# The opening of a fused attention and gated-FFN kernel: root scratch in PSUM, scalings on ScalarE, another order of the first loads, fewer warm-up matmuls

## The chip, the cores and the metric

The kernel runs on one core of one Trainium2 chip, as a single program with one launch. The metric is the device time of one execution in microseconds (us). The core has five engines with queues of their own, each worked off in order: TensorE (PE in the profile; PEld is its weight load), VectorE (DVE), ScalarE (ACT), GpSimd (POOL) and SyncE (SP), which here only issues DMAs. ACT issues a few DMAs too.

## What is computed

The input x is one sequence of 2048 tokens of width 512 in float32. It is normalised (mean and variance of a token, without gain), and two branches work on the result: attention with 32 heads of 16 columns and a window of 256 tokens, and a gated FFN of width 1792. Cut to its core, the reference is:

```python
xn = (x - mean(x)) / sqrt(var(x) + 1e-5)
q, k, v = split(xn @ wqkv)                 # 32 heads of 16
p = softmax(where(0 <= i - j < 256, q @ k.T / 4, -1e9))
s = (p @ v) @ wo
g = silu((silu(xn @ w_gate) * (xn @ w_up)) @ w_down)
out = x + s * g
```

## The kernel before

**Arithmetic.** Every float32 operand of a dense product is split in two parts of the format float32r: a high part (ACT casts it) and a low part, the difference (POOL for weights, DVE for what comes out of PSUM). Three products are made of them, high by high, high by low and low by high. All dense matmuls stand on line 580 (`mm`). In names, `wr` is a raw weight tile, `wh` and `wl` its parts, `xh` and `xl` those of x, and `xt` a raw tile of 128 tokens by 512 columns.

**Two halves.** PE's 128 rows are used as two halves of 64 that work on different matmuls at the same time. A unit of dense work (`vp` values, `a` queries and keys, `g` and `u` gate and up, `d` down, `s` the output product) runs on its lower half first (row half 0), and later the other 64 rows add into the same PSUM bank (row half 1). Between them stands a handover, line 577: a one-column copy by DVE that reads the bank after half 0 has finished, and for which half 1's first matmul waits. Half 0 of a unit uses the lower rows of its weight tile, half 1 the upper rows of the next tile.

**The order.** The whole program is straight-line code written by a planner in Python: it keeps a virtual clock, estimated costs of each instruction (`do`, `dma`) and due times, and emits each instruction when the virtual clock says that its inputs are there. The order on each engine is fixed by it; on the chip an engine waits only at semaphores. Dense units come from a list that `dense_order` sorts with the constant `LEAD`; attention work (`b` row maxima, `mt` and `ms` their turn and negation, `c` scores, `pv`) is slotted between by due times that are counted in dense work less the same `LEAD`.

**The opening.** `load_first` (line 320) fetches the first 512 tokens as four tiles `xt` in row halves over the queues of SP and ACT, and the first weights, those of the value product (`wr0`, `wr1`). DVE takes mean and variance of each tile (lines 338 and 339); the tiles are centred, two by ACT (346) and two by DVE (343). PE turns the centred tiles with matmuls against an identity (`x_turn`, line 442) into PSUM banks `xp`, ACT casts the high part (465), DVE subtracts for the low part (462). The value product of these centred, not yet scaled tokens starts at once, and its result is scaled when it leaves PSUM (838). Meanwhile DVE finds the reciprocal root of the four variances: two `tensor_scalar` for variance plus epsilon (`ve`, 362) and its half (`hv`, 363), an integer shift and subtraction for a first guess (364, 365), and three Newton steps of three instructions each (370 to 372), all on 128 x 4 elements. Then the x tiles are scaled (two by DVE on 387, two by ACT on 385) and turned once more in 64-row halves (`xt_turn`, line 600) for all later products. Until the first x tile is there, PE runs matmuls on a constant tile (`warm_up`, line 242): 20 at the start, 3 and 5 more behind the first two turns. A float32 matmul of this kind shows as two passes in the profile.

**The constants.** Three key buffers need rows of ones. `constants2` fetches them by nine DMAs from a tile of ones (`k<-one`) on SP's queue. Weights after the first come by `w_fetch`, a chain that begins at virtual time 4.0.

## Time and profile before

| | us |
|---|---|
| median of 3 runs | 863.81 (863.65 to 864.82) |
| the profiled execution, its own time | 866.53 |
| its span in the profile | 864.4 |
| PE busy | 852.1 |
| DVE, ACT, POOL busy | 509.7, 484.9, 627.2 |
| mean granted TensorE clock | 0.994 |

The profiled execution took 2.1 us more than its span, and 2.7 us more than the median of the runs without a profile. "Busy" counts the time in which at least one matmul was in work, so a PE that runs on one half of its rows counts as fully busy. In the views, a row of the timeline gives start, length, engine, line, operation, what is written and read, shapes, and in brackets the idle time before it with what ended it. A row of the windows gives the stretch, its length, the busy time with the number of instructions, the granted TensorE clock, the DMA share and GB/s.

### The profile page before, as it was taken

To read this page: it belongs to the slowest core of one execution; us is meant where nothing else is said; L and a number is where in the kernel's file an instruction comes from. 1 tells how busy PE (TensorE), PEld (TensorE's weight loads), DVE (VectorE), ACT (ScalarE), POOL (GpSimd) and SP (SyncE) were. 2 spreads that over 40 slices of the span, in tenths; PEclk is the share of its full clock that TensorE was granted. 3 is DMA by queue.
4 is the path that set the end of the run, shared out by engine and by line. 5 is a ranking of instruction groups with operands and counts; after the bars stand their busy time and mean duration, and the time that the engine had idled before them with its cause. 6 is when DMAs were issued, how large, how long until landed. Compare 5 with 4: busy or idle time off the path is not lost.

```text
span 864.4 us, 30040 instructions
## 1 busy us (share of the span) xinstructions
PE 852.1 (99%) x11976; PEld 794.6 (92%) x11976; DVE 509.7 (59%) x1672; ACT 484.9 (56%) x966; POOL 627.2 (73%) x906
## 2 busy tenths in 40 slices
PE   7999999999999999999999999999999999999997
PEld 7998988889999989989999998999999999999897
DVE  6337576655766565756657776566555576653234
ACT  4624755655666447655566656565546665665430
POOL 6535867877777587868787788667677877888770
PEclk9999999999999999999999999999999999999999
DMA  7279847475876986487758977666777778845241
GB/s 180 76 177 186 214 117 195 126 197 128 184 172 163 240 210 156 89 204 167 185 112 196 224 188 182 137 167 139 178 173 195 148 179 175 193 109 139 79 132 50
DMA packets 69550, 139.61 MB, mean 162 GB/s; under 512 B 14610, under 2 KB 23314, under 8 KB 69412
## 3 DMA queue, kind: packets, MB, share of 16 engines
q1 hardware_dynamic: 69092, 137.18, 66.4%
q8 instruction: 94, 1.54, 0.8%
q10 hardware_dynamic: 320, 0.52, 0.2%
q14 instruction: 44, 0.36, 0.2%
HBM read 107.74 MB, written 29.62 MB: 159 GB/s over the span
## 4 chain that ended last, share of the span: by engine, by line
PE 89%; DMA 7%; DVE 1%; SPq 1%; ACT 0%; issue 0%; POOL 0%; ACTq 0%; POOLq 0%; DVEq 0%
PE u L580 17%; PE d L580 17%; PE g L580 17%; PE a L580 10%; PE pv L1285 8%; PE c L1248 6%; PE b L1100 5%; PE vp L580 5%; PE s L580 4%; DMA xt<-x 1%; SPq L100 1%; DMA r<-rd 1%; DMA out<-y 1%; DMA qkd<-qkl 1%; DMA q<-ms 1%; DMA wr<-wv 1%
## 5 line engine op out<-in xcount | busy, mean ns | idle before, releaser
L545 POOL TENSOR_TENSOR wl<-wr,wh 128x512 fp32r<-128x512 f32 (+2 forms) x258 | 304.5, 1195 | 94.9 <-ACT wh L541 81.5
L1108 DVE CUSTOM_DVE_ANT_0 jk<-b,maskb 128x384 bf16<-128x384 f32 (+2 forms) x512 | 271.6, 530 | 103.1 <-PE b L1100 50.5
L580 PE MATMUL d<-wh,hh 64*128 64x256 f32 x1792 | 262.1, 278 | 0.0
L1208 ACT ACTIVATE p<-c 128x512 f32<-128x512 f32 (+2 forms) x384 | 197.6, 571 | 98.9 <-PE c L1248 95.0
L580 PEld LDWEIGHTS d<-wh,hh 64*128 64x128 f32 x1792 | 227.6, 185 | 1.1 <-issue 0.6
L580 PE MATMUL d<-wl,hh 64*128 64x256 f32 x896 | 208.4, 278 | 0.0
L580 PE MATMUL u<-xh,wl 64*128 64x512 f32 x448 | 168.3, 394 | 0.0
L580 PE MATMUL u<-xh,wh 64*128 64x512 f32 x448 | 168.2, 396 | 0.0
L580 PE MATMUL g<-xh,wh 64*128 64x512 f32 x448 | 166.5, 394 | 1.2 <-DVE ho L577 1.2
L580 PE MATMUL u<-xl,wh 64*128 64x512 f32 x448 | 167.1, 394 | 0.0
L580 PE MATMUL g<-xl,wh 64*128 64x512 f32 x448 | 167.0, 395 | 0.0
L580 PE MATMUL g<-xh,wl 64*128 64x512 f32 x448 | 167.0, 394 | 0.0
L541 ACT ACTIVATE wh<-wr 128x512 fp32r<-128x512 f32 (+2 forms) x258 | 142.5, 589 | 36.7 <-DMA wr<-wgu 20.4
L580 PEld LDWEIGHTS d<-wl,hh 64*128 64x128 f32 x896 | 152.5, 185 | 0.7 <-issue 0.2
L1220 POOL TENSOR_SCALAR_AFFINE_SELECT p<-p 128x256 f32<-128x256 f32 x256 | 101.9, 410 | 25.0 <-ACT p L1208 24.8
L1100 PE MATMUL b<-k,q 48*128 48x384 f32 (+2 forms) x512 | 113.0, 328 | 1.2 <-ACT ms L1149 0.7
L1224 POOL TENSOR_SCALAR_AFFINE_SELECT p<-p 128x256 f32<-128x256 f32 x224 | 91.5, 409 | 28.5 <-ACT p L1208 28.2
L735 POOL TENSOR_TENSOR hh<-h,hh 128x512 fp32r<-128x512 f32 x56 | 72.4, 1293 | 36.9 <-ACT hh L731 36.8
L1248 PE MATMUL c<-q,k 49*128 49x128 f32 (+2 forms) x704 | 96.0, 299 | 0.2 <-DMA q<-ms 0.2
L580 PE MATMUL a<-xh,wh 64*128 64x512 f32 x256 | 95.2, 393 | 0.0
L580 PE MATMUL a<-xh,wl 64*128 64x512 f32 x256 | 95.2, 392 | 0.0
L580 PE MATMUL a<-xl,wh 64*128 64x512 f32 x256 | 94.9, 392 | 0.0
(112 smaller groups left out, 2154.9 us busy)
## 6 DMA issues: line engine op xcount, KB each, us to landing
wr<-wgu SPq DMA_DIRECT2D x112, 256.0 KB
k<-qkd SPq DMA_DIRECT2D x48, 192.0 KB
wr<-wqk SPq DMA_DIRECT2D x32, 256.0 KB
qkd<-qkh SPq DMA_DIRECT2D x32, 256.0 KB
qkd<-qkl SPq DMA_DIRECT2D x32, 256.0 KB
q<-qkd SPq DMA_DIRECT2D x64, 128.0 KB
wr<-wdn SPq DMA_DIRECT2D x32, 256.0 KB
od<-ev SPq DMA_DIRECT2D x32, 256.0 KB
```

The source lines that it names most:

```text
L100: eng.dma_start(dst, src)
L541: nc.scalar.activation(wtile[j][0][pr, a:b], raw[pr, a:b], AF.Copy)
L545: nc.gpsimd.tensor_tensor(lo[pr, a:b], raw[pr, a:b], f32(hi[pr, a:b]), op=ALU.subtract)
L580: return nc.tensor.matmul(pb, a, b, start=first, stop=last, skip_group_check=True)
L735: nc.gpsimd.tensor_tensor(hl[:, 1, :], self.h, f32(hl[:, 0, :]), op=ALU.subtract)
L1100: nc.tensor.matmul(pb[:, :n], qs[u % 3][r : r + 48, p, qb * P : (qb + 1) * P], ks[u % 3][r : r + 48, p, lo : lo + n], start=True, stop=True,)
L1108: nc.vector.tensor_tensor_reduce(junk[:, :n], pb[:, :n], maskb[:, 3 * P - n :], 1.0, -3.0e38, ALU.add, ALU.max, m[:, col : col + 1],)
L1208: nc.scalar.activation(t[:, h, :], pc[:, :n], AF.Exp, scale=DH ** -0.5)
L1220: nc.gpsimd.affine_select(s, s, [[0, 2], [1, P]], ALU.is_ge, 0.0, base=0, channel_multiplier=-1)
L1224: nc.gpsimd.affine_select(s, s, [[0, 2], [-1, P]], ALU.is_gt, 0.0, base=0, channel_multiplier=1)
L1248: nc.tensor.matmul(pc[:, at0 : at0 + w], ks[u % 3][r : r + 49, p, k0 : k0 + P], qs[u % 3][r : r + 49, p, qb * P : qb * P + w], start=(i == ...
L1285: nc.tensor.matmul(pbs[r][0][32 * j : 32 * j + 32, q0:q1], vt[half(r), (4 * c + kb) % VT, VW * (4 * g + j) : VW * (4 * g + j) + 32], t[hal ...
```

## The change

In words, from top to bottom of the diff:

- `LEAD` goes from 0.9 to 1.1, which moves units in the dense list and attention work between them, over the whole run.
- The rows of ones are fetched by three DMAs of 2 x 3 x 512 elements in place of nine of 2 x 512.
- The scratch of the roots (`ve`, `tm` and the running root `r1`) lies in the PSUM bank of the warm-ups, `wbank`; `hv`, a new product tile `t1` and the finished root `rs` lie in SBUF.
- Of the four x tiles, three are centred on ACT and one on DVE; all four are scaled on ACT.
- The first weight tile's lower rows come in two column halves, one on ACT's queue and one on SP's, ahead of the third x tile; the fourth x tile and the upper rows of the second weight tile come over SP alone, the latter in column halves.
- The third and fourth x tile are turned into banks of the dense pool (`fb_free`) in place of the attention pool (`rb_free`).
- Warm-ups go from 20, 3 and 5 to 11, 1 and 2, and the weight chain begins at virtual time 6.5.
- The planner's numbers for landings, engines and lanes in the opening are changed with them.

```diff
@@ -50,7 +50,7 @@
 PRIO = -0.5
 MM = 0.2315
 PACE = 17.6
-LEAD = 0.9
+LEAD = 1.1
 OUT = 2.4
 STEP = 0.05
 LAND = 3.5
@@ -212,17 +212,17 @@
         for t in mts:
             nc.gpsimd.memset(t, 0.0)
 
-        def ones(t, b):
+        def ones(t):
             k = t[48 : 113 : 64].rearrange("p a n -> p (a n)")
-            move(k[:, b * 512 : b * 512 + 512], one[:2])
+            move(k.rearrange("p (b n) -> p b n", b=3), one[:2].unsqueeze(1).to_broadcast([2, 3, 512]))
 
         def done(t, i):
             ones_at[i] = t
-            if i == 8:
+            if i == 2:
                 timer(t, give, one)
 
-        for i in range(9):
-            dma(max(now[0], 1.1), lambda i=i: ones(ks[i // 3], i % 3), lambda t, i=i: done(t, i), 4.0, 8)
+        for i in range(3):
+            dma(max(now[0], 1.1), lambda i=i: ones(ks[i]), lambda t, i=i: done(t, i), 4.0, 8)
         nc.gpsimd.memset(vt[:, :, : H * VW].rearrange("p t (h c) -> p t h c", c=VW)[:, :, :, DH], 1.0)
         nc.gpsimd.memset(vt[:, :, H * VW :], 1.0)
 
@@ -318,18 +318,19 @@
     first = {}
 
     def load_first():
-        mv, ve, rs, tm, nm = (
+        mv, rs, nm = (
             pers.tile([P, 4, 2] if n == "mv" else [P, 4], F32, name=f"{n}0", tag=n)
-            for n in ("mv", "ve", "rs", "tm", "nm")
+            for n in ("mv", "rs", "nm")
         )
-        hv = pers.tile([P, 4], F32, name="hv")
+        hv, t1 = (pers.tile([P, 4], F32, name=n) for n in ("hv", "t1"))
+        ve, tm, r1 = (wbank[:, 256 + 4 * n : 260 + 4 * n] for n in range(3))
         first["rs"] = rs
         left = [4]
-        lands = (3.7, 4.7, 6.8, 7.8)
-
-        def rows(i):
+        lands = (3.8, 4.75, 6.4, 7.3)
+
+        def rows(i, upper):
             xt[0, i] = take(f"xt0_{i}")
-            for r, eng in ((0, nc.sync), (1, nc.scalar)):
+            for r, eng in ((1, upper), (0, nc.sync)):
                 at = i * P + R * r
                 move(xt[0, i][half(r)], x[at : at + R, :], eng)
 
@@ -337,7 +338,7 @@
             st = sb(f"st0_{i}", [P, 6], F32, "st", 2)
             nc.vector.bn_stats(st, xt[0, i])
             nc.vector.bn_aggr(mv[:, i, :], st)
-            if i % 2 == 0:
+            if i != 1:
                 nc.vector.tensor_scalar(nm[:, i : i + 1], mv[:, i, 0:1], -1.0, None, op0=ALU.mult)
             else:
                 nc.vector.tensor_scalar(xt[0, i], xt[0, i], mv[:, i, 0:1], None, op0=ALU.subtract)
@@ -349,8 +350,8 @@
             turns[i] = t
 
         def after_stats(t, i):
-            if i % 2 == 0:
-                do("S", t, 0.55, lambda: center(i), lambda t: centered(t, i), -1.0)
+            if i != 1:
+                do("S", t, 0.6, lambda: center(i), lambda t: centered(t, i), -1.0)
             else:
                 centered(t, i)
             left[0] -= 1
@@ -363,28 +364,25 @@
             nc.vector.tensor_scalar(hv, mv[:, :, 1], EPS, -0.5, op0=ALU.add, op1=ALU.mult)
             nc.vector.tensor_scalar(tm.bitcast(i32), ve.bitcast(i32), 1, None, op0=ALU.logical_shift_right)
             nc.vector.tensor_scalar(
-                rs.bitcast(i32), tm.bitcast(i32), -1, 0x5F3759DF, op0=ALU.mult, op1=ALU.add
+                r1.bitcast(i32), tm.bitcast(i32), -1, 0x5F3759DF, op0=ALU.mult, op1=ALU.add
             )
 
-        def newton():
-            nc.vector.tensor_tensor(tm, rs, hv, op=ALU.mult)
-            nc.vector.tensor_tensor(tm, rs, tm, op=ALU.mult)
-            nc.vector.scalar_tensor_tensor(rs, tm, 1.5, rs, op0=ALU.add, op1=ALU.mult)
+        def newton(n):
+            nc.vector.tensor_tensor(t1, r1, hv, op=ALU.mult)
+            nc.vector.tensor_tensor(t1, r1, t1, op=ALU.mult)
+            nc.vector.scalar_tensor_tensor(rs if n == 2 else r1, t1, 1.5, r1, op0=ALU.add, op1=ALU.mult)
 
         def step(t, n):
             if n < 3:
-                do("V", t, 0.6, newton, lambda t: step(t, n + 1), -0.5)
+                do("V", t, 0.6, lambda: newton(n), lambda t: step(t, n + 1), -0.5)
                 return
             rsready.append(t)
+            rb_free[wtag] = t
             for i in range(4):
-                e = "S" if i % 2 else "V"
-                do(e, t, 0.55, lambda i=i: scale(i), lambda t, i=i: normed.__setitem__((0, i), t), 0.1 * i)
+                do("S", t, 0.6, lambda i=i: scale(i), lambda t, i=i: normed.__setitem__((0, i), t), 0.1 * i)
 
         def scale(i):
-            if i % 2:
-                nc.scalar.activation(xt[0, i], xt[0, i], AF.Identity, scale=rs[:, i : i + 1])
-            else:
-                nc.vector.tensor_scalar(xt[0, i], xt[0, i], rs[:, i : i + 1], None, op0=ALU.mult)
+            nc.scalar.activation(xt[0, i], xt[0, i], AF.Identity, scale=rs[:, i : i + 1])
 
         def split(raw, j, r, t):
 
@@ -414,29 +412,32 @@
 
                 do("S", t, 0.53, lambda a=a: high(a), done, 0.3 + 0.001 * a)
 
-        rows(0)
-        rows(1)
+        rows(0, nc.scalar)
+        rows(1, nc.scalar)
         wr = [w_take(f"wr{j}", F32) for j in range(2)]
         u0, u1 = weighted[0], weighted[1]
-        for t, r, u, at in ((wr[0], 0, u0, 0), (wr[1], 1, u0, 1)):
-            move(t[half(r), : u.width], u.src[half(r)])
-        rows(2)
-        rows(3)
+        for a, eng in ((512, nc.scalar), (0, nc.sync)):
+            move(wr[0][half(0), a : a + 512], u0.src[half(0), a : a + 512], eng)
+        rows(2, nc.scalar)
+        rows(3, nc.sync)
+        for a in (0, 512):
+            move(wr[1][half(1), a : a + 512], u0.src[half(1), a : a + 512])
         move(wr[1][half(0), : u1.width], u1.src[half(0)])
         split_next[0] = 2
-        free_at["D"] = free_at["S"] = 4.0
-        stream_at[0] = 5.0
-        lanes[:] = [5.2, 5.8, 6.8, 6.8, 7.8, 7.8, 8.3, 8.3]
+        free_at["D"] = 6.8
+        free_at["S"] = 4.7
+        stream_at[0] = 5.7
+        lanes[:] = [5.4, 6.3, 6.4, 7.2, 7.3, 7.8, 8.2, 9.2]
         for i in range(4):
-            do("V", lands[i], 1.05 if i % 2 == 0 else 1.45, lambda i=i: stats(i), lambda t, i=i: after_stats(t, i), -1.0)
-        split(wr[0], 0, 0, 5.3)
-        split(wr[1], 1, 1, 7.2)
-        split(wr[1], 1, 0, 8.5)
+            do("V", lands[i], 1.05 if i != 1 else 1.45, lambda i=i: stats(i), lambda t, i=i: after_stats(t, i), -1.0)
+        split(wr[0], 0, 0, 5.5)
+        split(wr[1], 1, 1, 8.3)
+        split(wr[1], 1, 0, 9.3)
 
     def x_turn(i):
         h = i // 2
         if i % 2 == 0:
-            first["ab"[h]] = [bank(rb_free, f"xp0_{2 * h + n}") for n in range(2)]
+            first["ab"[h]] = [bank(fb_free if h else rb_free, f"xp0_{2 * h + n}") for n in range(2)]
         for k in range(KC):
             at = (k % 2) * 256 + (i % 2) * P
             nc.tensor.matmul(
@@ -445,10 +446,9 @@
             )
         advance(0.45)
         if i == 0:
-            warm_up(warm, 3)
+            warm_up(warm, 1)
         if i == 1:
-            warm_up(warm, 5)
-            rb_free[wtag] = now[0] + 0.6
+            warm_up(warm, 2)
         if i % 2 == 0:
             return
 
@@ -460,7 +460,7 @@
             def low(t):
                 cready[h, n] = t
                 do("V", t, 0.69, lambda: nc.vector.tensor_tensor(lo, src, f32(hi), op=ALU.subtract),
-                   lambda t: (rb_free.__setitem__(tag, t), lready.__setitem__((h, n), t)), 0.0)
+                   lambda t: ((fb_free if h else rb_free).__setitem__(tag, t), lready.__setitem__((h, n), t)), 0.0)
 
             do("S", now[0] + 0.2, 0.55, lambda: nc.scalar.activation(hi, src, AF.Copy), low, -0.5)
 
@@ -1192,7 +1192,7 @@
     def prob_ready(u, e, p):
         if p_place(2 * prob_cols(u, e)) is None:
             return None
-        return latest([ms_at.get(u), bank_time(rb_free, 2), p_freed[0], *(ones_at.get(u % 3 * 3 + n) for n in range(3))])
+        return latest([ms_at.get(u), bank_time(rb_free, 2), p_freed[0], ones_at.get(u % 3)])
 
     p_freed = [0.0]
 
@@ -1514,11 +1514,11 @@
     load_first()
     th0 = pers.tile([P, 1], F32, name="th0")
     nc.scalar.activation(th0, warm[:, :1], AF.Tanh)
-    warm_up(warm, 20)
+    warm_up(warm, 11)
     rb_free[wtag] = 99.0
     constants()
     free_at["G"] = 1.5
-    timer(4.0, w_fetch, 2)
+    timer(6.5, w_fetch, 2)
     plan_attention()
     constants2()
     marks.append((-LEAD + 0.1, load_qk, (0,)))
@@ -1531,7 +1531,7 @@
             fn(*a)
         pump()
         n = min((i for i in range(4) if i not in first), default=None)
-        if n is not None and turns.get(n, 99.0) <= now[0] and (n % 2 or latest([bank_time(rb_free, 2), now[0]]) == now[0]):
+        if n is not None and turns.get(n, 99.0) <= now[0] and (n % 2 or latest([bank_time(fb_free if n else rb_free, 2), now[0]]) == now[0]):
             first[n] = True
             x_turn(n)
             continue```

**DVE in the opening.** First what stands on DVE behind the statistics of the fourth tile before the change (`tm`, `ve`, `rs` and `hv` are the roots' scratch, `xp` the banks of turned x, `ho` the handover of the first value unit), then what stands there now, where the scratch in PSUM goes by the bank's name `warm` and `t` is `t1`.

```order
L462 TENSOR_TENSOR xl_82<-xp_0_164,xh_81 128x2x256
L462 TENSOR_TENSOR xl_82<-xp_1_165,xh_81 128x2x256
L362 TENSOR_SCALAR ve_89<-mv_88 128x4
L363 TENSOR_SCALAR hv<-mv_88 128x4
L364 TENSOR_SCALAR tm_91<-ve_89 128x4
L365 TENSOR_SCALAR rs_90<-tm_91 128x4
L370 TENSOR_TENSOR tm_91<-rs_90,hv 128x4
L371 TENSOR_TENSOR tm_91<-rs_90,tm_91 128x4
L372 SCALAR_TENSOR_TENSOR rs_90<-tm_91,rs_90 128x4
L577 COPY ho<-vp_0_0_194 80x1
```

```order
L363 TENSOR_SCALAR warm<-mv_88 128x4
L364 TENSOR_SCALAR hv<-mv_88 128x4
L365 TENSOR_SCALAR warm<-warm 128x4
L366 TENSOR_SCALAR warm<-warm 128x4
L462 TENSOR_TENSOR xl_82<-xp_1_155,xh_81 128x2x256
L371 TENSOR_TENSOR t_92<-warm,hv 128x4
L372 TENSOR_TENSOR t_92<-warm,t_92 128x4
L373 SCALAR_TENSOR_TENSOR warm<-t_92,warm 128x4
L371 TENSOR_TENSOR t_92<-warm,hv 128x4
L372 TENSOR_TENSOR t_92<-warm,t_92 128x4
L373 SCALAR_TENSOR_TENSOR warm<-t_92,warm 128x4
L577 COPY ho<-vp_0_0_183 80x1
```

The handover stands behind two Newton steps where it stood behind one, the roots begin between the two low parts of x, and of the roots only `hv` is written from SBUF to SBUF.

**ACT in the opening.** What stands on ACT from the first centring to the scalings, before and now (`xt` tiles being centred or scaled, `wh` the first weights' high parts, `xh` that of x).

```order
L346 ACTIVATE xt_0_94<-xt_0_94,nm_92 128x512
L394 ACTIVATE wh_161<-wr_100 64x512 x2
L465 ACTIVATE xh_81<-xp_0_164 128x2x256
L465 ACTIVATE xh_81<-xp_1_165 128x2x256
L346 ACTIVATE xt_2_104<-xt_2_104,nm_92 128x512
L394 ACTIVATE wh_208<-wr_101 64x512 x4
L465 ACTIVATE xh_81<-xp_2_214 128x2x256
L465 ACTIVATE xh_81<-xp_3_215 128x2x256
L541 ACTIVATE wh_265<-wr_159 128x512 x2
L385 ACTIVATE xt_1_97<-xt_1_97,rs_90 128x512
L385 ACTIVATE xt_3_107<-xt_3_107,rs_90 128x512
```

```order
L392 ACTIVATE wh_151<-wr_99 64x512 x2
L465 ACTIVATE xh_81<-xp_0_154 128x2x256
L347 ACTIVATE xt_2_103<-xt_2_103,nm_90 128x512
L465 ACTIVATE xh_81<-xp_1_155 128x2x256
L347 ACTIVATE xt_3_106<-xt_3_106,nm_90 128x512
L392 ACTIVATE wh_211<-wr_100 64x512 x3
L465 ACTIVATE xh_81<-xp_2_191 128x2x256
L465 ACTIVATE xh_81<-xp_3_192 128x2x256
L392 ACTIVATE wh_211<-wr_100 64x512
L385 ACTIVATE xt_0_93<-xt_0_93,rs_89 128x512
L385 ACTIVATE xt_1_96<-xt_1_96,rs_89 128x512
L385 ACTIVATE xt_2_103<-xt_2_103,rs_89 128x512
```

The centring of the third tile stands ahead of the high part of the first two tiles' second half (`xp_1`), the fourth tile's centring has come to ACT, and the casts of the third weight tile stand behind the four scalings (the fourth follows the last row shown).

**SP at the start.** What SP issues behind the first two x tiles, before and now (`wr_99`, `wr_100` and `wr_101` are the first weight tiles, `one` the tile of ones).

```order
L100 DMA wr_100<-wv 64x1024
L100 DMA wr_101<-wv 64x1024
L100 DMA xt_2_104<-x 64x512
L100 DMA xt_3_107<-x 64x512
L100 DMA wr_101<-wv 64x1024
L100 DMA wr_159<-wqk 64x1024
L100 DMA wr_159<-wv 64x1024
L100 DMA k_75<-one 2x512 x3
L100 DMA k_76<-one 2x512 x3
L100 DMA k_77<-one 2x512 x3
L100 DMA wr_286<-wqk 64x1024 x2
```

```order
L100 DMA wr_99<-wv 64x512
L100 DMA xt_2_103<-x 64x512
L100 DMA xt_3_106<-x 64x512 x2
L100 DMA wr_100<-wv 64x512 x2
L100 DMA wr_100<-wv 64x1024
L100 DMA k_75<-one 2x3x512
L100 DMA k_76<-one 2x3x512
L100 DMA k_77<-one 2x3x512
L100 DMA wr_189<-wqk 64x1024
L100 DMA wr_189<-wv 64x1024
L100 DMA wr_204<-wgu 64x1024
```

The third x tile stands one place behind 128 KB of weights, where it stood behind 512 KB of them, and the third weight tile follows the ones where it went ahead of them.

## The prediction

> **What bounds the kernel now.** I read the page first.
>
> ```profile
> span 864.4 us, 30040 instructions
> PE 852.1 (99%) x11976; PEld 794.6 (92%) x11976; DVE 509.7 (59%) x1672; ACT 484.9 (56%) x966; POOL 627.2 (73%) x906
> ```
>
> PE sets the end: 852.1 of 864.4 us. A gain must come out of the 12.3 us in which PE is idle, or out of time in which it is busy but slow. So I read the windows next (stretch, its length, PE's busy time and matmuls, granted clock, DMA share, GB/s), coarse ones over the run and fine ones at the start.
>
> ```profile
> 10.00:20.00 10.00, 6.53 (x49) 0.91 0.64 149
> 20.00:30.00 10.00, 9.85 (x138) 0.75 0.42 102
> 18.00:18.50 0.50, 0.00 (x0) 0.76 0.91 254
> 24.50:25.00 0.50, 0.50 (x10) 0.50 0.92 180
> 25.00:25.50 0.50, 0.50 (x12) 0.91 1.01 344
> 70.00:72.00 2.00, 0.75 (x8) 1.00 0.92 245
> 74.00:76.00 2.00, 1.29 (x13) 1.00 1.09 180
> ```
>
> Two things stand out. Between 10 and 20 us PE lacks 3.47 us. And between about 18.3 and 25.1 us the granted clock is 0.50, so PE is busy there at half its speed. After the opening only 1.25 and 0.71 us are lost near 70 us and a few tenths elsewhere, and at the end nothing that the change touches. The waits of PE and the timeline say what ends the gap.
>
> ```profile
> PE vp L580 <- DVE ho L577: 3.5, 1, 3.5
> 12.27 5.10 POOL L398 TENSOR_TENSOR wl<-wr,wh 64x512 fp32r<-64x512 f32 x4 [1.19 <-issue]
> 13.20 0.37 DVE L362 TENSOR_SCALAR ve<-mv 128x4 f32<-128x4 f32 x1
> 13.48 0.16 DVE L363 TENSOR_SCALAR hv<-mv 128x4 f32<-128x4 f32 x1
> 13.60 1.20 DVE L364 TENSOR_SCALAR tm<-ve 128x4 int32<-128x4 int32 x1
> 15.04 3.58 DVE L370 TENSOR_TENSOR tm<-rs,hv 128x4 f32<-128x4 f32 x1
> 16.34 0.28 PE L580 MATMUL vp<-wl,xh 64*128 64x256 f32 x1
> 17.34 2.47 POOL L545 TENSOR_TENSOR wl<-wr,wh 128x512 fp32r<-128x512 f32 x2
> 18.65 1.19 DVE L371 TENSOR_TENSOR tm<-rs,tm 128x4 f32<-128x4 f32 x1
> 19.95 0.15 DVE L577 COPY ho<-vp 80x1 f32<-80x1 f32 x1
> 20.15 0.58 PE L580 MATMUL vp<-wh,xh 64*128 64x256 f32 x1 [3.54 <-DVE ho L577]
> 20.61 0.15 DVE L370 TENSOR_TENSOR tm<-rs,hv 128x4 f32<-128x4 f32 x1
> 30.65 0.39 PE L580 MATMUL a<-xh,wh 64*128 64x512 f32 x1
> ```
>
> The same DVE instruction on four columns takes 3.58 us at 15.04 and 0.15 us at 20.61. The difference is POOL: its subtractions run from 12.27 without a pause to 19.81, three DVE instructions are stretched in that time (1.20, 3.58, 1.19 us), and none after it. The handover, which needs nothing of the roots, stands behind them. Half 1 of the first value unit cannot start, PE's queue is in order, and PE stops at 16.62. At 18.26 the clock falls to half and it is full again only at 25.09 (the shares 0.76 and 0.91 of the half microseconds in which it changes).
>
> **The sum.** I follow the change by PE's milestones: the first matmul of the second value unit (14.70 before), the first of half 1 (20.15), the first of `a` (30.65), from which on the order is dense in both kernels.
>
> ```profile
> 1.10 6.39 PE L242 MATMUL warm<-warm 128*128 128x128 f32 x40 [1.10 <-DVE warm L237]
> 4.93 0.69 DVE L338 BATCH_NORM_STATS2 st<-xt 128x6 f32<-128x512 f32 x1
> 5.04 0.72 ACT L346 ACTIVATE xt<-xt,nm 128x512 f32<-128x512 f32 x1 [0.24 <-DVE nm L341]
> 5.88 0.49 DVE L343 TENSOR_SCALAR xt<-xt,mv 128x512 f32<-128x512 f32 x1
> 7.86 1.15 ACT L394 ACTIVATE wh<-wr 64x512 fp32r<-64x512 f32 x2 [2.10 <-DMA wr<-wv]
> 7.93 5.98 SPq L100 DMA_DIRECT2D k<-one  x9
> 9.63 0.69 DVE L338 BATCH_NORM_STATS2 st<-xt 128x6 f32<-128x512 f32 x1 [3.26 <-DMA xt<-x]
> 10.08 0.50 PE L580 MATMUL vp<-wh,xh 64*128 64x256 f32 x2
> 10.76 0.73 ACT L346 ACTIVATE xt<-xt,nm 128x512 f32<-128x512 f32 x1 [0.79 <-DVE nm L341]
> 11.51 2.33 ACT L394 ACTIVATE wh<-wr 64x512 fp32r<-64x512 f32 x4
> 12.00 1.28 DVE L462 TENSOR_TENSOR xl<-xp,xh 128x512 fp32r<-128x512 f32 x2
> 13.74 1.05 ACT L465 ACTIVATE xh<-xp 128x512 fp32r<-128x512 f32 x2
> 14.70 0.39 PE L580 MATMUL vp<-wh,xh 64*128 64x256 f32 x2
> ```
>
> *Second value unit.* Eleven warm-ups in place of twenty end at 4.6 (11/20 of 6.39, from 1.10) to 5.5 (the early ones are the slow ones); the first tile is centred at 5.76, so they hold up nothing. The second is centred at 6.37. The first weights' landing released ACT at 7.86; at that place in SP's queue 512 KB had gone before its end, now 384 KB stand there, and DVE began on the tile before it at 4.93 without a wait, so I take 6.2 (an estimate between 4.9 and 7.86). Two casts (1.15), one high part of x (half of 1.05): the first value matmul at 7.9, where it stood at 10.08. The next link is the third x tile. It landed at 9.6; its SP half now ends at the 512 KB where the weights ended (7.86), its ACT half comes fourth as an x half did before. I take 8.1, bounds 6.4 and 9.6. From landing to centred it was 9.63 to 11.49, 1.86: centred at 10.0. ACT then does one high part (10.5), the fourth tile's centring (0.73, 11.2), three weight casts (2.33/4 each, 12.9), and the next high part (13.4): second value unit at 13.45, **1.25 us earlier**. The wait that I add is on ACT: the centring waits for a landing, and the second high part, the fourth tile and all weight casts are queued behind it, PE behind those. With a landing at 9.6 the term is -0.25, with 6.4 it is 2.9 at most. The centring that DVE gave up (0.49) costs ACT 0.73 and is in this chain.
>
> *The stall.* From 14.70 to 16.5, where half 1's first matmul is due, 15 matmuls pass; so it is due at 15.2 now. DVE has by then: statistics to 10.4, two low parts (1.28), four root instructions and six of Newton at about 0.2 from start to start (the product at 20.61 takes 0.15; of PSUM operands the trace has the handover, 0.15 too, so I take no more for the scratch there, and at most the 0.37 that L362 took): 13.7, and the handover 13.9. At 0.37 each it would be 1.7 later, 0.4 us of stall. At 0.2 it is 1.3 us early: **3.65 us** (20.15 less 16.5). The cover is that 1.3 us. Without it each microsecond of DVE delay costs one. What remains exposed is `hv`, still SBUF to SBUF beside POOL: 0.16 in the row above, 1.20 if it meets what L364 met, which the cover holds.
>
> [...]
>
> *The clock.* From 20.15 to 25.09 PE worked 4.94 us at half clock; at full clock that is 2.47 us of work: **2.47 us**. Half 1's start at 15.2 leaves 15.2 + 10.50 - 2.47 = 23.2 for the first `a`, 7.4 before 30.65.
>
> *What the rebuilt part takes back.* Four scalings one after the other on ACT cost 2.6 us, where each engine took two (22.26 to 23.59 on ACT):
>
> ```profile
> L385 ACT ACTIVATE xt<-xt,rs x2: 710/716/723, 22.3 to 22.9; 128x512 f32<-128x512 f32 x2
> L387 DVE TENSOR_SCALAR xt<-xt,rs x2: 475/480/486, 22.3 to 23.4; 128x512 f32<-128x512 f32 x2
> ```
>
> The last root is due at 15.1, so the last scaling ends at 17.7; the turns on line 600 stand 24 half-1 matmuls behind 15.2, at 18.0. Nearly covered, 0 to 1. The third weight tile's casts now come behind the scalings (18.3), POOL's two subtractions (2.47) end near 22.0, and the unit that reads them is due at 22.4: 0 to 1. I take 0.4 for both. The weights themselves are no issue: six fewer DMAs of ones take 2 us of SP where nine took 5.98. The dense banks for the last x tiles cost nothing: the pool has four, and the unit that would want a fifth starts after the low parts have freed two.
>
> *`LEAD`.* It reorders the run, with the same matmuls: the 128-row passes of warm-ups aside, nothing is added. The stalls that a new order could remove are the 1.96 us near 70 and 0.7 elsewhere; as many could be new. I take 0, bounds -2.7 and +2.7, an estimate by what the old order has.
>
> Sum: 1.25 + 3.65 + 2.47 - 0.4 = **7.0 us**. The profiled execution took 866.53 (span 864.4 and 2.1 around it), so 859.5 for its like; the median of the runs stands 2.7 lower at 863.81, so **856.8 us**. The likeliest case alone spans 855.0 to 858.5.
>
> **Rivals.**
>
> *The clock falls all the same (17%).* PE stopped at 16.62 and the clock fell at 18.26, 1.64 us later, after a stretch in which only half 0 worked. The new opening has gaps too: by my times 7.3 to 7.9 and 8.5 to 10.0, and half 0 alone until 15.2. Against it: the idle 1.25 us near 70 cost no clock. If it falls near 11, for the 6.8 us of before, PE's work in it is about half of them and part of the loss falls into waits: 2.5 us, 859.3. [...]
>
> *POOL still holds the roots (8%).* If `hv` is held as long as L370 was (3.58), 1.3 of it is covered; 2.3 us of stall come back, and 859.1 follows. For it: it is the one SBUF pair left. Against: its 0.16.
>
> *Given back at the next transfers (10%).* Near 70 us PE waited for DVE and ACT, and these for weights:
>
> ```profile
> 69.18 4.26 DMA wr<-wqk
> 73.53 1.15 ACT wh L541 x2
> 60.00:80.00 20.00, 18.05 (x160) 1.00 0.90 175
> ```
>
> With a DMA share of 0.90 there, a PE that comes 7 us earlier may meet the same transfers at the old time. Half given back: 860.3. Against it: the weight chain leaves SP earlier, and the DMA share between 30 and 60 us has room.
>
> *Slower (7%).* The new order can put weight casts that wait for DMAs ahead of ACT's attention work, as at 73.53, which cost 1.96 us of PE for one. From four such places on (7.8) the gain is gone; five give 863.8 - 7.0 + 9.8 = 866.6.
>
> *The change doesn't do what it says (3%).* If it is the issue of small instructions and not the shared SBUF side that stretches the roots, PSUM scratch keeps the stall: 863.8. The 0.15 at 20.61 speaks against it.
>
> **How the numbers follow.** Forecast 55%, the rivals 17, 8, 10, 7 and 3. Within 0.2% (1.7 us, about what a measurement of this kernel can tell from no change) lie the last rival and part of the given-back one; faster: 55 + 17 + 8 and most of 10, 0.88; same 0.06; slower 0.06. The range takes in the rivals up to a half given back, and below the forecast the earliest landing and the order's bound: 853.8 to 861.0.
>
> **What will show it.** Right: roots of about 0.2 us each between 11 and 15 us; the handover before 15; no PE gap above 1 us after the second value unit; full clock to the end; first `a` at 22.5 to 24. Wrong: a first `a` after 26, a clock of 0.50 between 8 and 20, or, with an early `a`, PE gaps of more than 5 us between 40 and 100.

## The result, and the profile after

The changed kernel took 853.86 us (median of 5 runs, 852.53 to 855.05) where the kernel before took 864.82 in the same comparison (5 runs, 863.65 to 867.18): a ratio of 0.9872, with a 95% interval of 0.9851 to 0.9892. That is 11.0 us less; the forecast was 7.0. The ratio makes 852.8 of the 863.81 from which the forecast was worked out, a microsecond below the low end of its range. The profiled execution took 853.76, as the median; the one of before, at 866.53, lay 1.7 above the median of these runs, so spans differ by more (12.4) than medians.

The page's head, and the waits of PE (engine and line, waited for; us in total, times, longest):

```profile
span 852.0 us, 29940 instructions
PE 845.1 (99%) x11948; PEld 795.6 (93%) x11948; DVE 502.1 (59%) x1670; ACT 488.8 (57%) x969; POOL 628.8 (74%) x906
```

```profile
PE warm L242 <- DVE warm L237: 1.1, 1, 1.1
PE xp L443 <- ACT xt L347: 0.6, 1, 0.6
PE c L1248 <- DMA q<-ms: 0.3, 1, 0.3
```

The handover no longer stands in this list, and behind the opening one wait of 0.3 is left. The timeline shows the opening (start, length, engine, line; the scratch tile in PSUM goes by the bank's name, `warm`, the root lines stand one further down than before, those of the weight parts two further up):

```profile
8.40 0.50 PE L580 MATMUL vp<-wh,xh 64*128 64x256 f32 x2
10.66 0.17 DVE L365 TENSOR_SCALAR warm<-warm 128x4 int32<-128x4 int32 x1
11.54 0.15 DVE L371 TENSOR_TENSOR t<-warm,hv 128x4 f32<-128x4 f32 x1
11.56 5.12 POOL L396 TENSOR_TENSOR wl<-wr,wh 64x512 fp32r<-64x512 f32 x4 [1.71 <-ACT wh L392]
11.73 0.16 DVE L372 TENSOR_TENSOR t<-warm,t 128x4 f32<-128x4 f32 x1
11.92 0.17 DVE L373 SCALAR_TENSOR_TENSOR warm<-t,warm 128x4 f32<-128x4 f32 x1
13.58 0.40 PE L580 MATMUL vp<-wh,xh 64*128 64x256 f32 x2
13.78 0.15 DVE L577 COPY ho<-vp 80x1 f32<-80x1 f32 x1 [1.10 <-PE vp L580]
14.83 0.16 DVE L373 SCALAR_TENSOR_TENSOR rs<-t,warm 128x4 f32<-128x4 f32 x1
15.08 2.56 ACT L385 ACTIVATE xt<-xt,rs 128x512 f32<-128x512 f32 x4 [0.99 <-DVE rs L373]
23.35 0.39 PE L580 MATMUL a<-xh,wh 64*128 64x512 f32 x1
```

POOL subtracts from 11.56 to 16.68, and in that very time Newton's steps take 0.15 to 0.17 us each. The handover is through at 13.93, the first `a` starts at 23.35 where it started at 30.65. The windows (stretch, length, busy time of PE, PEld, DVE, ACT, POOL, granted clock, DMA share, GB/s) answer to those of before:

```profile
10.00:20.00 10.00, 10.00 (x131) 9.53 (x131) 5.12 (x21) 8.96 (x20) 6.34 (x5) 1.00 0.95 223
20.00:30.00 10.00, 10.00 (x142) 9.71 (x140) 2.79 (x10) 7.42 (x18) 6.68 (x6) 1.00 0.45 99
70.00:72.00 2.00, 2.00 (x22) 1.97 (x20) 1.82 (x7) 1.39 (x3) 1.05 (x2) 1.00 0.34 106
74.00:76.00 2.00, 2.00 (x22) 1.63 (x20) 1.11 (x5) 1.94 (x4) 2.00 (x2) 1.00 0.04 8
60.00:80.00 20.00, 20.00 (x186) 19.16 (x184) 13.58 (x54) 12.80 (x28) 15.00 (x20) 1.00 0.58 146
```

131 matmuls in the second 10 us (49 before), the clock stays full, and the two stalls near 70 us are gone too. So up to the first `a` the change is worth 7.3 us, where 7.0 was forecast. What is to be explained is the rest, 3.7 of the 11.0: it arises later, where the instructions are the same in kind and only their order is new.

### The profile page after: what moved, and what is told of

The parts are those of the page before. It is cut to its first block, busy times and chain, and to the rows that moved or that the text cites. A ratio compares the mean times of both kernels' runs of the same rounds, so it can differ in the third digit from the quotient of the medians.

```text
span 852.0 us, 29940 instructions
## 1 busy us (share of the span) xinstructions
PE 845.1 (99%) x11948; PEld 795.6 (93%) x11948; DVE 502.1 (59%) x1670; ACT 488.8 (57%) x969; POOL 628.8 (74%) x906
## 3 DMA queue, kind: packets, MB, share of 16 engines
q8 instruction: 94, 1.54, 0.8%
## 4 chain that ended last, share of the span: by engine, by line
PE 97%; DMA 1%; DVE 0%; ACTq 0%; ACT 0%; issue 0%; DVEq 0%
PE u L580 19%; PE g L580 19%; PE d L580 19%; PE a L580 10%; PE pv L1285 8%; PE c L1248 6%; PE s L580 6%; PE vp L580 5%; PE b L1100 5%; DMA q<-ms 1%; DMA xt<-x 1%; PE xp L600 1%; ACTq L100 0%; PE mt L1134 0%; PE xp L443 0%; ACT xt L347 0%
## 5 line engine op out<-in xcount | busy, mean ns | idle before, releaser
L545 POOL TENSOR_TENSOR wl<-wr,wh 128x512 fp32r<-128x512 f32 (+1 forms) x258 | 305.3, 1197 | 83.1 <-ACT wh L541 63.6
L1108 DVE CUSTOM_DVE_ANT_0 jk<-b,maskb 128x384 bf16<-128x384 f32 (+2 forms) x512 | 271.5, 530 | 103.2 <-PE b L1100 62.6
L580 PE MATMUL d<-wh,hh 64*128 64x256 f32 x1792 | 266.9, 279 | 0.0
L580 PEld LDWEIGHTS d<-wh,hh 64*128 64x128 f32 x1792 | 228.2, 185 | 1.1 <-issue 0.6
L580 PE MATMUL d<-wl,hh 64*128 64x256 f32 x896 | 205.2, 278 | 0.0
L580 PE MATMUL g<-xh,wl 64*128 64x512 f32 x448 | 158.6, 395 | 0.0
L580 PE MATMUL g<-xh,wh 64*128 64x512 f32 x448 | 157.4, 392 | 0.0
L580 PE MATMUL u<-xh,wl 64*128 64x512 f32 x448 | 157.3, 393 | 0.0
L580 PE MATMUL u<-xh,wh 64*128 64x512 f32 x448 | 157.0, 393 | 0.0
L580 PE MATMUL g<-xl,wh 64*128 64x512 f32 x448 | 157.0, 392 | 0.0
L580 PE MATMUL u<-xl,wh 64*128 64x512 f32 x448 | 156.8, 393 | 0.0
L541 ACT ACTIVATE wh<-wr 128x512 fp32r<-128x512 f32 (+1 forms) x258 | 142.7, 589 | 17.3 <-PE d L580 5.7
L580 PEld LDWEIGHTS d<-wl,hh 64*128 64x128 f32 x896 | 145.8, 185 | 0.3
L1100 PE MATMUL b<-k,q 48*128 48x384 f32 (+2 forms) x512 | 111.4, 328 | 0.0
L580 PE MATMUL a<-xl,wh 64*128 64x512 f32 x256 | 96.7, 390 | 0.0
L580 PE MATMUL a<-xh,wl 64*128 64x512 f32 x256 | 96.4, 391 | 0.0
L580 PE MATMUL a<-xh,wh 64*128 64x512 f32 x256 | 96.2, 392 | 0.0
L1248 PE MATMUL c<-q,k 49*128 49x128 f32 (+2 forms) x704 | 95.8, 299 | 0.3 <-DMA q<-ms 0.3
```

What stands on the lines that cost most here:

```text
L541: nc.scalar.activation(wtile[j][0][pr, a:b], raw[pr, a:b], AF.Copy)
L545: nc.gpsimd.tensor_tensor(lo[pr, a:b], raw[pr, a:b], f32(hi[pr, a:b]), op=ALU.subtract)
L580: return nc.tensor.matmul(pb, a, b, start=first, stop=last, skip_group_check=True)
L1100: nc.tensor.matmul(pb[:, :n], qs[u % 3][r : r + 48, p, qb * P : (qb + 1) * P], ks[u % 3][r : r + 48, p, lo : lo + n], start=True, stop=True,)
L1108: nc.vector.tensor_tensor_reduce(junk[:, :n], pb[:, :n], maskb[:, 3 * P - n :], 1.0, -3.0e38, ALU.add, ALU.max, m[:, col : col + 1],)
L1248: nc.tensor.matmul(pc[:, at0 : at0 + w], ks[u % 3][r : r + 49, p, k0 : k0 + P], qs[u % 3][r : r + 49, p, qb * P : qb * P + w], start=(i == ...
```

## The experiments

Sixteen kernels were run. For an order of instructions I use one number that needs no run, the **order sum**: PE's matmuls laid end to end in their order, each for its width at the trace's rate, the two halves beside each other. It is 747.5 for the kernel before and 746.9 for the changed one. It counts what is lost when one half works alone, and no waits.

| run | what it is | median us | ratio to before, 95% |
|---|---|---|---|
| e1_lead_alone | before, `LEAD` 1.1 | 865.83 | 1.0011, 0.9998 to 1.0025 |
| e2_lead_back | changed, `LEAD` 0.9 | 858.54 | 0.9913, 0.9894 to 0.9932 |
| e3_roots_sbuf | changed, root scratch in SBUF | 860.24 | 0.9935, 0.9911 to 0.9958 |
| e4_warm_20 | changed, 20/3/5 warm-ups | 855.63 | 0.9886, 0.9866 to 0.9907 |
| e5_warm_0 | changed, one warm-up | 860.10 | 0.9936, 0.9911 to 0.9961 |
| e6_lead_100 | changed, `LEAD` 1.0 | 861.47 | 0.9952, 0.9937 to 0.9968 |
| e7_lead_120 | changed, `LEAD` 1.2 | 862.71 | 0.9975, 0.9963 to 0.9986 |
| e8_old_lead_100 | before, `LEAD` 1.0 | 875.95 | 1.0137, 1.0105 to 1.0168 |
| e9_ones_back | changed, nine DMAs of ones | 864.87 | 0.9996, 0.9980 to 1.0013 |
| e10_scale_split | changed, two scalings on DVE | 863.23 | 0.9977, 0.9961 to 0.9993 |
| e11_old_faults | changed, e3 and e4 together | 860.75 | 0.9934, 0.9911 to 0.9957 |
| e12_prio_60 | changed, `PRIO` -0.6 | 853.80 | 0.9861, 0.9832 to 0.9890 |
| e13_pad | changed, an unused tile | 856.17 | 0.9897, 0.9875 to 0.9920 |
| e14_old_pad | before, an unused tile | 865.18 | 0.9999, 0.9985 to 1.0013 |
| e15_prio_70 | changed, `PRIO` -0.7 | 856.58 | 0.9902, 0.9879 to 0.9925 |
| e16_roots_sbuf_pad | e3 with the unused tile | 861.28 | 0.9954, 0.9937 to 0.9971 |

Each ratio is to the kernel before on the same chip (864.8 to 865.8). The prices below are differences of medians; by the ratios they come out up to 1.5 us smaller.

### Is the rest `LEAD`, or the opening?

```diff
 # e1_lead_alone, on the kernel before
-LEAD = 0.9
+LEAD = 1.1
 # e2_lead_back, on the changed kernel
-LEAD = 1.1
+LEAD = 0.9
```

> The kernel before with LEAD = 1.1 and nothing else. Theory L (the order that LEAD makes takes away the stalls behind the opening, about 4.5 us of the 11): 860.3 us, about 0.995 of before, and the PE gaps of 1.25 and 0.71 us between 70 and 76 us are gone, the opening unchanged (first matmul of a near 30.7). Rival D (the stalls went because the opening brings its weights earlier, LEAD does nothing): 864.8, with gaps near 70 us as before.

> The changed kernel with LEAD = 0.9 as before. Theory L: the opening keeps its 7.7 us (first matmul of a near 23.2), about 4.5 us of stalls come back behind it: 858.4. Rival D: 853.9, no PE gap above 0.5 us between 40 and 340 us.

`LEAD` alone gains nothing (865.83, where theory L had 860.3), and the new opening without it gains 6.3 us (858.54, where theory L had 858.4). The second number was met, but not for the reason given: the stalls that were to come back did not. The stall near 70 us, 1.95 us idle in these 20 us before, went in both. The window of e1_lead_alone:

```profile
60.00:80.00 20.00, 19.93 (x177) 18.55 (x175) 16.59 (x68) 8.31 (x16) 11.93 (x11) 1.00 0.78 187
```

and that of e2_lead_back:

```profile
60.00:80.00 20.00, 20.00 (x186) 19.15 (x186) 13.77 (x55) 10.82 (x23) 13.72 (x18) 1.00 0.97 222
```

So either change alone removes the stall: it hangs on the order, not on the old opening or the old `LEAD` by itself (another order behind the old opening, e8_old_lead_100 below, has it again). Both runs lost again further on what they had won there. Counted in matmuls done, e2_lead_back was 10.3 us ahead of before at 122 us and 8.6 at 302, without a wait of PE above 0.3; its order sum is 749.6, 2.7 above that of the changed kernel. e1_lead_alone idles by 0.18 us from 60 to 800 us, where before has 2.69, and still its span is only 0.5 shorter; no order sum of it is on record. That gave theory O: whatever touches the opening or a constant draws the whole order anew, and orders differ by more than I allowed.

### The parts of the opening, with the order held fixed

These four kernels keep every instruction behind the opening in the order of the changed kernel.

```diff
 # e3_roots_sbuf
-        ve, tm, r1 = (wbank[:, 256 + 4 * n : 260 + 4 * n] for n in range(3))
+        ve, tm, r1 = (pers.tile([P, 4], F32, name=n) for n in ("ve0", "tm0", "r1"))
 # e4_warm_20: 20, 3 and 5 warm-ups for 11, 1 and 2; e5_warm_0: 1, 0 and 0
-    warm_up(warm, 11)
+    warm_up(warm, 20)
 # e11_old_faults: both edits of e3_roots_sbuf and e4_warm_20
```

> The changed kernel with ve, tm and r1 in SBUF tiles in place of the PSUM bank, in the same order of instructions. Theory P (DVE instructions with both tensors in SBUF wait for POOL's subtractions): the Newton rows that fall between 11.6 and 16.7 us are stretched to 1.2 us and more each, the handover comes after 16 in place of 13.8, PE gets a gap of 1 to 4 us and perhaps half clock: 856 to 860. Rival S (it is the small instructions, wherever they lie): no row above 0.4 us, 853.9.

> The changed kernel with 20, 3 and 5 warm-ups as before, in an otherwise equal order. Theory W (the warm-ups stand in PE's queue ahead of the turns and hold the chain up): first value matmul at 9.6 to 10.1 in place of 8.4, second value unit 0.8 to 1.3 us later, 854.7 to 855.2. Rival: the third x tile's centring ends later than the warm-ups, so nothing: 853.9.

> The changed kernel, with its order and LEAD = 1.1, but with the two faults of the old opening put back together: roots scratch in SBUF (alone +6.4) and the 20, 3 and 5 warm-ups (alone +1.8). It is the nearest to the old opening under the new order. Theory O (the opening and the order behind it are two separate gains): first `a` at 27 to 28, no stall near 70 us, and 853.9 + 6.4 + 1.8 = 862.1, 860.5 to 864; a window of 3.41 us in which PE idles by over 1.5 us, if the handover's wait makes one, lets the clock fall and adds 1.7. Theory D (the stall near 70 us goes only because the opening ends earlier): PE idles again near 70 us and the time is 864.5 to 866.5.

> The changed kernel with one warm-up matmul at the start and none behind the turns; order behind it unchanged. Theory G (the clock is raised and lowered after stretches of 3.41 us by how much of each PE was at work): PE is idle until about 7, so the clock stays half until a stretch with more than half of it at work, at 10 to 17 us; the matmuls up to there take double, the handover comes 0.5 to 3 us later and the time is 855 to 857.5. Rival: warm-ups only fill time and the time is 853.9.

**Roots in SBUF** cost 6.4 us by the medians (856 to 860 was expected, 860.24 came). In the profiled execution, whose mean clock is 0.999 as in the changed kernel, it is 4.3. The other three executions show 0.997; the difference is what one window at half clock makes (half of 3.41, 1.7 us), as seen in e16_roots_sbuf_pad below. The timeline of the profiled one, where POOL's four subtractions run from 11.25 to 16.32:

```profile
11.23 0.15 DVE L371 TENSOR_TENSOR t<-r,hv 128x4 f32<-128x4 f32 x1
11.25 5.07 POOL L396 TENSOR_TENSOR wl<-wr,wh 64x512 fp32r<-64x512 f32 x4 [1.41 <-ACT wh L392]
11.42 1.11 DVE L372 TENSOR_TENSOR t<-r,t 128x4 f32<-128x4 f32 x1
12.57 1.19 DVE L373 SCALAR_TENSOR_TENSOR r<-t,r 128x4 f32<-128x4 f32 x1
16.27 0.14 DVE L577 COPY ho<-vp 80x1 f32<-80x1 f32 x1
16.46 0.38 PE L580 MATMUL vp<-wh,xh 64*128 64x256 f32 x1 [1.22 <-DVE ho L577]
```

Same instructions, same engine, same neighbours as in the changed kernel: only the place of `r` moved from PSUM to SBUF, and 0.16 became 1.11. The two stretched rows end at 12.53 and 13.76, about where POOL's first two subtractions end (four in 5.07 us: 12.52 and 13.79). That settles why the Newton steps were slow: the place of the operands, not the issue of small instructions. What it is that DVE and POOL share on the side of SBUF, as the prediction has it, no run shows. The shift on L364 of the kernel before, with one SBUF input and 1.20 us beside POOL, was not tested: in the changed kernel and in e3_roots_sbuf the first four root instructions ran while POOL stood idle.

**Warm-ups.** Twenty of them delay the first value matmul to 10.72 (9.6 to 10.1 was expected) and the second value unit to 15.2, and the end follows: +1.8 by the medians, 1.4 by the spans (0.8 to 1.3 was expected). One alone costs 6.2: in e5_warm_0 no record of a full clock stands before 21.39 us (the windows print 1.00 where no record exists yet, so the matmuls themselves must be read). Start to start on one half they take 0.21 until then and 0.12 behind it:

```profile
20.61 0.41 PE L576 MATMUL vp<-wh,xh 64*128 64x256 f32 x1
20.82 0.41 PE L576 MATMUL vp<-wl,xh 64*128 64x256 f32 x1
21.44 0.28 PE L576 MATMUL vp<-wh,xh 64*128 64x256 f32 x1
21.56 0.28 PE L576 MATMUL vp<-wl,xh 64*128 64x256 f32 x1
```

I had given 855 to 857.5, for a rise behind the first stretch with more than half of it at work; that half was a guess, and no run shows it. What I had not foreseen stands in two windows of 3.41 us (both print 1.00, for the reason given): in the first, half 0 works alone and PE is busy throughout (3.42 us), and the clock does not rise behind it; in the second, half 1 joins at about 19.4, and it rises.

```profile
14.56:17.98 3.42, 3.42 (x18) 3.42 (x18) 0.72 (x3) 0.57 (x2) 2.00 (x2) 1.00 1.04 231
17.98:21.39 3.41, 3.41 (x27) 3.41 (x28) 1.02 (x5) 2.56 (x4) 0.00 (x0) 1.00 1.04 223
```

Eleven warm-ups lie between two prices.

**Both old faults together** cost 6.9 (860.75; I had given 862.1, 860.5 to 864), with no stall near 70 us. Of these only 3.25 us stand at the first `a` (26.60; 27 to 28 was expected). The delay then grew to 7.0 at the end, with PE's instructions in the same order and no new wait above 0.5 us. e3_roots_sbuf grew likewise from 2.3 to 4.3 us, while e4_warm_20 (1.6 to 1.4) and e5_warm_0 (5.4 to 5.1) did not grow. In these two the opening's delay passes through to the end about one for one; why it grew in the runs with roots in SBUF was asked next.

### Is it where the tiles lie?

The three small tiles in SBUF shift what is allocated behind them. An unused tile of 32 bytes shifts it alone:

```diff
 # e13_pad (on the changed kernel) and e16_roots_sbuf_pad (on e3_roots_sbuf)
-        hv, t1 = (pers.tile([P, 4], F32, name=n) for n in ("hv", "t1"))
+        hv, t1, _ = (pers.tile([P, 4], F32, name=n) for n in ("hv", "t1", "pad"))
 # e14_old_pad (on the kernel before)
-        hv = pers.tile([P, 4], F32, name="hv")
+        hv, _ = (pers.tile([P, 4], F32, name=n) for n in ("hv", "pad"))
```

> The changed kernel with one tile of 32 bytes a partition added that nothing writes or reads; every instruction is the same and stands in the same order. It moves what is allocated behind it by 32 bytes: 179 of the 242 tiles of weight parts then begin at 32 bytes past a multiple of 64, as 181 of them do in the kernel before and 179 in the run with roots in SBUF; in the changed kernel it is 63. Theory A (the place of the tiles in SBUF is worth the part of the gain that neither opening nor order explains): 855.9 to 858, the difference growing along the run as it did with roots in SBUF (2.3 behind the opening, 4.3 at the end). Rival: 853.9 within 0.8.

> The kernel before with the same unused tile of 32 bytes: instructions and order as before, and 181 of 242 weight tiles begin at a multiple of 64 bytes where 61 did. Theory A: 861 to 863 in place of 864.8. Rival: 864.8 within 0.8.

> The changed kernel with the roots' scratch in SBUF and the unused tile of 32 bytes, so that the tiles behind it begin where they do in the changed kernel (179 of 242 weight tiles at a multiple of 64). Theory A: only the delay of the opening is left, 853.9 + 2.3 = 856.2, 855.5 to 857. Rival (the roots in SBUF cost 6.4 however the tiles lie): 860.2, 859 to 861.5.

Theory A, that it matters whether a tile begins at a multiple of 64 bytes, falls with two of the three. The kernel before does not gain (0.9999), and roots in SBUF cost as much with the tiles back in place (861.28 and not 856.2; 1.7 of it is the clock, below). The third does not decide: the median of e13_pad (856.17) lies in the range of theory A, but its interval overlaps that of the changed kernel, and its profiled execution has a span of 852.1 against 852.0. With the same instructions its first `a` came at 22.54 and its median 2.3 us higher; so a milestone of one execution is good to about 0.8 us, and some 2 us between two of these kernels say little. What makes the delay grow stays open. It grew between the first `a` and the end in all four kernels whose tiles were moved at all (e3_roots_sbuf 2.0, e11_old_faults 3.7, e16_roots_sbuf_pad 3.0, e13_pad 0.9 us) and in neither of the two whose tiles were not (e4_warm_20, e5_warm_0); a place effect other than the 64 bytes is not excluded. Part of the price of e16_roots_sbuf_pad is the clock: at the handover's wait of 1.2 us it fell for one window (the second row), which it had not in the profiled execution of e3_roots_sbuf:

```profile
14.29:17.70 3.41, 2.08 (x20) 1.67 (x19) 3.31 (x8) 0.07 (x1) 2.10 (x2) 1.00 1.04 231
17.70:21.12 3.42, 3.42 (x34) 3.42 (x32) 0.59 (x2) 3.01 (x5) 0.28 (x1) 0.50 1.04 226
```

### How much do orders differ?

Seven kernels with new orders, six of them behind the new opening. `PRIO` (line 50) is the planner's priority for the work of DVE and ACT that empties the banks of dense units:

```diff
 # e6_lead_100, on the changed kernel (e7_lead_120: 1.2; e8_old_lead_100: 1.0 on the kernel before)
-LEAD = 1.1
+LEAD = 1.0
 # e12_prio_60, on the changed kernel (e15_prio_70: -0.7)
-PRIO = -0.5
+PRIO = -0.6
 # e9_ones_back
-        for i in range(3):
-            dma(max(now[0], 1.1), lambda i=i: ones(ks[i]), lambda t, i=i: done(t, i), 4.0, 8)
+        for i in range(9):
+            dma(max(now[0], 1.1), lambda i=i: ones(ks[i // 3], i % 3), lambda t, i=i: done(t, i), 4.0, 8)
...
-    timer(6.5, w_fetch, 2)
+    timer(4.0, w_fetch, 2)
 # e10_scale_split (scale(i) then runs on DVE for tiles 0 and 2)
-                do("S", t, 0.6, lambda i=i: scale(i), ...
+                do("VS"[i % 2], t, 0.6, lambda i=i: scale(i), ...
```

> The changed kernel with LEAD = 1.0 (between the 0.9 and the 1.1 that have been run), nothing else. For every program I lay PE's matmuls end to end in their order, each for its width at the rate of the trace, the two halves beside each other and each start no earlier than that of the matmul ahead: this order sum is 746.9 for the changed kernel, 749.6 for it with LEAD 0.9, and 750.8 here. Theory O (the order sum, drawn anew by whatever touches the opening or LEAD, is what the rest of the gain hangs on): 853.9 + 3.9 = 857.8, 856.3 to 859.3, with no stall near 70 us and the first `a` at 23.0 to 23.5. Theory L (an earlier start of the casts is worth time as such, so the effect is steady in LEAD): between the two neighbours, 855.5 to 857.0, about 856.2.

> The changed kernel with LEAD = 1.2, nothing else. Order sum 752.6, 5.7 above the changed kernel's. Theory O: 853.9 + 5.7 = 859.6, 858.1 to 861.1, first `a` at 23.0 to 23.5, and the loss spread behind 100 us, not in waits of PE. Theory L: steady in LEAD, so 1.2 is no slower than 1.1: at most 854.5, or with a saturated lead 853.9.

> The kernel before with LEAD = 1.0. Order sum 749.9, 2.4 above the 747.5 of the kernel before. Theory O: the opening stays (first `a` at 30.7); 864.8 + 2.4 = 867.2 if the stall near 70 us stays, 864.6 if it goes as it did with 1.1; so 864 to 868. Theory D (the stall near 70 us hangs on when the weights come, so on the opening): the stall stays, as it should have with 1.1 and did not. Theory L: between 0.9 and 1.1, 864.8 to 865.8.

> The changed kernel with the nine DMAs of ones in place of three, and the weight fetch's timer back at 4.0; LEAD stays 1.1. The scheduler then draws another order: order sum 750.6, 3.7 above the changed kernel's. Theory O: the opening is hardly touched (first `a` at 23 to 23.8) and the time is 853.9 + 3.7 = 857.6, 856 to 859.5. Theory D (the fewer DMAs bring the weights earlier, and that is what removed the stall near 70 us): PE idles again near 70 us by 1.5 to 3 us, and the time is 859 to 861.5.

> The changed kernel with two of the four scalings back on DVE; LEAD stays 1.1. The scalings end 1.2 us earlier (about 16.4) and the first turns of x are no longer just behind them, but the turns wait for 24 matmuls of half 1 anyway: first `a` within 0.4 of 23.2. The scheduler draws another order, order sum 748.8, 1.9 above the changed kernel's. Theory O: 855.8 plus whatever stalls the new order has between 270 and 520 us, 0 to 6: 855 to 862. Rival (moving the scalings to ACT is itself worth the unexplained 4 us): first `a` 1 us later or more, and 858 with no new stall behind the opening.

> The changed kernel with another constant of the planner, PRIO = -0.6 for -0.5: the opening and all up to about 50 us are instruction for instruction the same, the order behind it differs. Order sum 747.25, 0.35 above. Theory O: 854.2 plus its stalls, 853.5 to 858; it says that nothing in LEAD is special and that an order's own stalls (PE waiting for casts, matrices or DMAs between 270 and 520 us) and the clock drops they cause are what separates orders of equal sum. Rival (853.9 belongs to LEAD = 1.1 and its earlier casts as such): within 0.5 of 853.9.

> The changed kernel with PRIO = -0.7 for -0.5: one more order behind the same opening, order sum 747.24, 0.34 above. Theory O: 854.2 plus the stalls this order has, 853.5 to 860; a wait of PE above 1 us, if there is one, between 270 and 520 us. Rival (orders of equal sum take equal time): 853.5 to 855.

In all those on the changed kernel the first `a` starts between 23.1 and 23.5 us. The opening is the same, and still the medians run from 853.8 to 864.9: e9_ones_back gives the whole gain back, with a first `a` at 23.34. Theory L falls: 1.0 and 1.2 are 7.6 and 8.9 us slower than 1.1, and 1.0 slower than 0.9. Theory O had the direction and was too low each time (857.8 for 861.5, 859.6 for 862.7, 857.6 for 864.9, 864 to 868 for 876.0), because the new orders also stall. Theory D falls with e9_ones_back, whose PE is busy for all of 60 to 80 us, and the rival in e10_scale_split with its first `a` at 23.20; in e8_old_lead_100, behind the old opening, PE idles by 1.71 us there again, which theory D had right for that run. What the orders differ by shows in a view of PE from 60 to 800 us, first of the kernel before, then of the changed one:

```profile
60.00:800.00 740.00, 737.31 (x10626) 685.49 (x10625) 460.57 (x1558) 438.36 (x877) 564.82 (x843) 1.00 0.72 170
```

```profile
60.00:800.00 740.00, 739.72 (x10739) 696.52 (x10737) 456.76 (x1539) 443.23 (x883) 570.97 (x847) 1.00 0.70 168
```

and of e6_lead_100, with its waits, and e9_ones_back, with its own:

```profile
60.00:800.00 740.00, 735.92 (x10582) 688.90 (x10580) 454.76 (x1536) 436.59 (x872) 562.99 (x841) 1.00 0.69 167
```

```profile
PE b L1100 <- ACT wh L541: 1.9, 1, 1.9
PE c L1248 <- DVE m L1108: 1.3, 2, 0.8
```

```profile
60.00:800.00 740.00, 736.40 (x10568) 692.34 (x10566) 451.65 (x1529) 436.31 (x873) 559.27 (x837) 1.00 0.71 166
```

```profile
PE s L580 <- issue: 1.9, 1, 1.9
PE vp L580 <- issue: 1.5, 1, 1.5
```

PE idles 0.28 us in the changed kernel (740.00 less 739.72), 2.69 before, 4.08 and 3.60 here. In e9_ones_back the clock fell twice as well, each time for one window of 3.41 us, 1.7 us of work lost. With the order sum this accounts for most of each span:

| order behind the new opening | order sum | PE idle, 60 to 800 us | clock lost | these three, over the changed kernel's | span, over the changed kernel's |
|---|---|---|---|---|---|
| changed kernel | 746.9 | 0.28 | 0 | 0 | 0 |
| e12_prio_60 | 747.25 | 0.12 | 0 | 0.2 | 0.3 |
| e15_prio_70 | 747.24 | 1.50 | 0 | 1.6 | 2.0 |
| e2_lead_back | 749.6 | 0.66 | 0 | 3.1 | 3.6 |
| e6_lead_100 | 750.8 | 4.08 | 0 | 7.7 | 9.3 |
| e7_lead_120 | 752.6 | 1.79 | 0 | 7.2 | 8.8 |
| e10_scale_split | 748.8 | 5.05 | 0 | 6.7 | 9.7 |
| e9_ones_back | 750.6 | 3.60 | 3.4 | 10.4 | 11.7 |
| kernel before, plus 7.3 for its opening | 747.5 | 2.69 | (in the 7.3) | 10.3 | 12.4 |

Up to 3 us of a row stay unexplained; PE counts as idle only when both halves are, and each span is that of one execution (that of the kernel before lay 1.7 above the median). e8_old_lead_100 fits in the same way against the kernel before: 2.4 in the order sum, 4.3 idle and 1.7 for a second fall of the clock make 8.4 of its 10.7. e12_prio_60 and the changed kernel cannot be told apart, and no order run was better. e12_prio_60 fits both of the expectations written for it; e15_prio_70 fits theory O, without a wait of PE above 1 us.

## Why the prediction was right about the opening and too small in all

**The second value unit** started at 13.58: 1.12 us earlier, 1.25 forecast. The first value matmul was due at 7.9 and came at 8.40. That the warm-ups would hold up nothing was right for eleven, but barely: they ended at 6.16 and not by 5.5, the first tile was centred at 6.25. e4_warm_20 shows that twenty would have held up this chain by 1.6, all of the term.

**The stall and the clock.** From the second value unit to the first `a` it was 15.95 us before and 9.77 after: 6.2 saved, where 3.65 + 2.47 - 0.4 = 5.7 was forecast. The handover was due at 13.9 and ran at 13.78; the last root was due at 15.1 and ended at 14.99, each Newton instruction taking 0.15 to 0.17 where about 0.2 from start to start was an estimate; the scalings were due to end at 17.7 and ended at 17.64. `hv`, the one instruction left exposed, took 0.16, but by luck it was not put to the test: it ran at 10.53, while POOL stood idle (9.86 to 11.56). The 0.4 taken back did not show. First `a`: 23.2 forecast, 23.35 measured. e3_roots_sbuf confirms by undoing it what the place of the scratch does beside POOL (0.16 us, and 1.11 in SBUF).

**The step that failed is `LEAD`**: "the same matmuls ... as many could be new. I take 0, bounds -2.7 and +2.7". The new order was worth about -3.7 us (11.0 less 7.3; by the last row of the table, 0.6 in the order sum and 2.4 in idle time account for 3.0, and 0.7 stays open). The mechanism named there, stalls removed or new ones made, was right, and near 70 us the removed ones were those that it counted. The size was wrong twice. Taking 0 set a removed stall against an equal new one, and the bounds were taken from the stalls that the old order had, which says nothing of what a new one can lose: orders drawn behind this same opening lie 0 to 11 us above the changed kernel. And "the same matmuls" hid that an order has a length of its own without any wait; between the orders run here it differs by 5.7 us.

**The constant is not the cause.** `LEAD` as such is not worth 4 us, as e1_lead_alone, e6_lead_100 and e7_lead_120 show; the value 1.1 behind this opening happens to give a short order without stalls. That part of the gain was luck. Of eight orders run behind the new opening only two reach 854.

**The rivals.** The clock did not fall: full from 6.98 to 850.07 us. In e16_roots_sbuf_pad it did, with 1.33 us idle in a window. POOL held no root, as far as any met it. Nothing was given back at the transfers near 70 us in the changed kernel, but giving back is real: e9_ones_back lost the whole gain, 6.8 us of it by two waits near 280 and 500 us with the falls of the clock behind them and 3.7 by a longer order, and its price was of the size that I gave to the slower rival, for another cause. What stays open: the growth of the delay with roots in SBUF, so the split of the 11.0 into 7.3 and 3.7 rests on the milestones, while e11_old_faults puts 6.9 on two parts of the opening; and up to 3 us in the rows of the table.

## What to carry to other kernels

Where a planner writes the order, an edit anywhere draws a new order, and its luck is a term of its own: bound it by building a few neighbours (other values of the same constant) and comparing what their orders cost without waits, not by the stalls of the old order. What the orders cost without waits is a lower bound: most of the new ones here stalled too. To learn what an edit is worth in itself, undo it with the order held fixed. Try a VectorE scratch in PSUM where GpSimd works beside it and something urgent is queued behind it: here it took a Newton instruction from 1.11 us to 0.16, and the wait at the handover (1.2 us in e3_roots_sbuf) was gone.
